# Six products a step instead of ten, and three reciprocals of a stage's four formed on ScalarE as exp(-ln)

## The chip, the cores and the metric

The kernel runs on one core of a Trainium2 chip, in one launch. The metric is the device time of that launch in microseconds (us), the median over several runs. The core has a matrix engine (PE, with its weight loads listed apart as PEld), VectorE (DVE), ScalarE (ACT), GpSimd (POOL), and SyncE (SP), which issues nearly all DMAs here. Each engine works through its own queue in order; they wait for one another by semaphores.

## The reference, cut to what matters

Input `A_x` is 2048 tokens by 640 features, 32 heads of 20. Two attention branches are computed from it and mixed by a per-token gate. The change lies in the first branch, A:

```python
qkv = (x @ wqkv) ...                       # q, k, v: 32 heads x 2048 tokens x 20
pq, pk = q @ w_phi, k @ w_phi              # per head, 20 x 20
phi_q = concat([softmax(pq), softmax(-pq)])   # 40 features of a head; phi_k likewise
kv  = einsum('sf,sd->fd', phi_k, v)        # 40 x 20 per head
z   = phi_k.sum(s)
num = phi_q @ kv                           # 2048 x 20 per head
den = phi_q @ z + 1e-6
a   = (num / den) @ wo
out = g * a + (1 - g) * b                  # g = sigmoid(x . gate_w); b is the second branch
```

Branch B is a causal attention in four segments of 512 tokens with a memory carried from one to the next. It comes after branch A's stage in the program and takes over half of the time.

## The kernel before, in words

The feature axis (640) is cut into five tiles of 128 rows, numbered j. A head has 20 rows, so heads straddle tiles: heads 6, 12, 19 and 25 have rows in two tiles. The 32 heads' results lie in two banks of PSUM, 16 heads (320 columns) each. `PIECES` (L63) lists the matmuls that put one row of heads together: (tile j, bank, first head, end head). Before, a head that two tiles share has a piece of its own (20 columns) in the second tile, so there are ten pieces, 36 heads' widths in all (720 columns). `FIRST` and `LAST` mark the pieces that open and close a bank.

`PIECES` is used in two places. `emit_foldM` (L186) folds `w_phi` into the key and query weights at the start of the program, five times for the keys (`WkA`) and five times for the queries (`WqA`). `emit_num` (L477) computes the numerators of 128 tokens ("chunk" `ch`, 16 of them) for one sign of the features (`sgn`, 2): 32 steps. A step's tile `num` has two banks; columns 0 to 319 of each hold the numerators. In the chunks 1, 5 and 9 the columns from 320 on also take the denominators of two later chunks (`emit_den`, L495: 20 small matmuls, 10 for each chunk), by both signs those of the next four chunks.

The stage around the change runs from about 88.8 to 127 us. Its order is written out by hand (a manual schedule). Four chunks are a batch; k is a chunk's place in it. For a step i = 2 ch + sgn, in the order of emission:

- DVE multiplies the numerators by a per-head factor into `tt` (`emit_tt`, L531). The factor of a batch's chunks is made one batch ahead.
- PE projects one half of a row of the second branch's keys, queries or values (`emit_half`, five matmuls of 320 columns, L561); ACT copies it out of PSUM (L621). There are two buffers for that (`pps`).
- PE computes the numerators of step i + 3 (L482), with denominators (L500) where they fall due. The three tiles `nps0`, `nps1`, `nps2` go round, so step i + 3 needs that everything which reads step i's tile is done.
- After both signs POOL adds the two halves of `tt` into `oA` (L691), and SP turns `oA` with a DMA. There are two `tt` tiles, so `tt` of chunk ch waits for `oA` of chunk ch - 2.

The factor of the next batch: on DVE, a reciprocal of one half of the denominators straight from PSUM into `rr` (L507) and a product with the other half into `uu` (L508), both right behind `tt` in the two steps of k = 1; the sum of `uu` over the signs, `dd` (L512), behind `tt` of step (k = 2, sign 0); at the end of k = 2 a reciprocal of `dd` (L694); then POOL multiplies by the gate (L522) and into `rr` (L524), behind `oA` of that chunk. The first batch's factor is made before the stage, from a tile `z_den`, in one piece (`first_chain`).

In chunks 1, 5, 9 and 11 ACT also starts exponential features of the keys (L706, L679, L681), which POOL adds two chunks later (L701).

Before the loop a short sequence fills the pipeline, L658: `"nnhhn"`, n for the numerators of the next step, h for a half. The stage's PSUM pools (`nps0`, `nps2`, `pps`, `nps1`, two banks each) take over the four two-bank tiles of the stage before, whose last work is a projection `pq` that ACT reads twice for its exponentials `Eq` (L428).

ACT loads its table of functions once, ahead of a dummy exponential (L132); until the end it runs exponentials, copies and Relu.

Of the kernel before, what the change touches and what calls it, by code (L numbers as in the profile page):

```python
# [7 lines left out]
ACT = mybir.ActivationFunctionType  # L8
ALU = mybir.AluOpType
BF16 = mybir.dt.bfloat16  # L10
F32 = mybir.dt.float32
# [4 lines left out]
def kernel(  # L16
# [15 lines left out]
    nc = tc.nc  # L32
    P = 128
    S = 2048
    D = 640
    H = 32
# [23 lines left out]


    TH = [(P * j // DH, (P * j + P - 1) // DH + 1) for j in range(KC)]
    PIECES = [(0, 0, 0, 7), (1, 0, 6, 7), (1, 0, 7, 13), (2, 0, 12, 13), (2, 0, 13, 16),  # L63
              (2, 1, 16, 20), (3, 1, 19, 20), (3, 1, 20, 26), (4, 1, 25, 26), (4, 1, 26, 32)]
    FIRST, LAST = {0, 5}, {4, 9}
    HW = 8

    gS = res.tile([P, NCH], F32, name="gS")
# [31 lines left out]
    for what in "c w1 w3 x0 x1 g v0 v1".split():  # L100
        n = int(what[1:]) if len(what) > 1 else 0
# [19 lines left out]
    for g in range(3):  # L121
# [7 lines left out]
                            compare_op=ALU.not_equal, fill=1.0, base=0,  # L129
                            channel_multiplier=1)  # L130
    nc.gpsimd.memset(tiny, 0.0)
    nc.scalar.activation(out=tiny, in_=tiny, func=ACT.Exp)  # L132
    wmask = Aw.tile([P, KC, H], F32, name="wmask")
    nc.gpsimd.memset(wmask, 1.0)
# [41 lines left out]
    def w2tile(name):  # L176
        return aps.tile([P, 2, 512], F32, name=name, tag="w2")
# [8 lines left out]
    def emit_foldM(WT, dst, ic, eng=nc.scalar.copy):  # L186
        ps = w2tile("fold_ps")
        for n, (j, bk, lo, hi) in enumerate(PIECES):
            h0 = TH[j][0]
            nc.tensor.matmul(ps[:, bk, (lo - 16 * bk) * DH:(hi - 16 * bk) * DH],  # L190
                             lhsT=WT[:, j, ic * P:(ic + 1) * P],
                             rhs=Wphi[:, j, lo - h0:hi - h0, :].rearrange("p h d -> p (h d)"),
                             start=(n in FIRST), stop=(n in LAST))
        eng(out=dst[:, ic, :].rearrange("p (b n) -> p b n", b=2), in_=ps[:, :, 0:320])

    def emit_xT(n):
# [120 lines left out]
    for step in "P T0a T2d M0a T1d M2a T4d T3d M1a X0 M4a X1 M3a k0 g k1 v0 v1 r0 r1".split():  # L317
        n = int(step[1:2] or 0)
# [29 lines left out]
    for n in range(KC):  # L348
# [12 lines left out]
        out=xg, in0=vA[:, :, 0, 320].rearrange("p (g u) -> p u g", u=4)[:, :, :, None].to_broadcast([P, 4, 4, 4]),  # L361
        in1=bd01[:, None, None, :].to_broadcast([P, 4, 4, 4]), op=ALU.mult)
# [101 lines left out]
    a3w = a3_stack.enter_context(tc.tile_pool(name="a3w", bufs=2, side="right", reuse_waits="tile"))  # L464
# [10 lines left out]
    NB = 4  # L475

    def emit_num(ch, sgn):  # L477
        qb, qc = divmod(ch, HB // P)
        t = nps[(2 * ch + sgn) % 3].tile([P, 2, 512], F32, name="num")
        for n, (j, bk, lo, hi) in enumerate(PIECES):  # L480
            h0 = TH[j][0]
            nc.tensor.matmul(t[:, bk, (lo - 16 * bk) * DH:(hi - 16 * bk) * DH],  # L482
                             lhsT=Eqs[qb, j][:, sgn, qc * P:(qc + 1) * P],
                             rhs=kvn[:, sgn, j, lo - h0:hi - h0, :].rearrange("p h e -> p (h e)"),
                             start=(n in FIRST), stop=(n in LAST))
        return t

    def num_view(t):
        return t[:, :, 0:320].rearrange("p b (h e) -> p b h e", e=DH)

    def den_view(t):

        return t[:, :, 320:448].rearrange("p n (s h e) -> p n s h e", s=2, e=2)
# [11 lines left out]
    def emit_rr(rr, uu, t, o, n):  # L505
        k = slice(o, o + n)
        nc.vector.reciprocal(out=rr[:, k], in_=t[:, :, :, :, 1])  # L507
        nc.vector.tensor_tensor(out=uu[:, k], in0=t[:, :, :, :, 0], in1=rr[:, k], op=ALU.mult)  # L508

    def emit_dsum(uu, n):  # L510
        dd = a3w.tile([P, NB, H], F32, name="dd", bufs=1)
        nc.vector.scalar_tensor_tensor(out=dd[:, 0:n], in0=uu[:, 0:n, 0, :], scalar=1e-6,  # L512
                                       in1=uu[:, 0:n, 1, :], op0=ALU.add, op1=ALU.add)
        return dd

    def rr_tiles():
        return (a3w.tile([P, NB, 2, H], F32, name="rr"), a3w.tile([P, NB, 2, H], F32, name="uu", bufs=1))

    def emit_cs(chs, rr, dd, o=0):
        n = len(chs)  # L520
        k = slice(o, o + n)
        nc.gpsimd.tensor_tensor(out=dd[:, k], in0=dd[:, k],  # L522
                                in1=gS[:, chs[0]:chs[0] + n, None].to_broadcast([P, n, H]), op=ALU.mult)
        nc.gpsimd.tensor_tensor(out=rr[:, k], in0=rr[:, k],  # L524
                                in1=dd[:, k, None, :].to_broadcast([P, n, 2, H]), op=ALU.mult)
        for i, ch in enumerate(chs):
            cs_of[ch] = rr[:, o + i]

    def emit_tt(tt, sgn, ps, cs):
        csb = cs[:, sgn].rearrange("p (b h) -> p b h", b=2)[:, :, :, None].to_broadcast([P, 2, 16, DH])  # L530
        nc.vector.tensor_tensor(out=tt[:, sgn].rearrange("p (b h) d -> p b h d", b=2),  # L531
                                in0=ps, in1=csb, op=ALU.mult)
# [52 lines left out]
    for what in "ppppvzppppdvp":  # L585
# [15 lines left out]
        name=n, bufs=2 if n == "pps" else 1, space=bass.MemoryType.PSUM, reuse_waits="tile"))  # L601
# [23 lines left out]
    def emit_turn(part, sc, dst):  # L625
        c = sc % 4
        nc.sync.dma_start_transpose(out=dst[:, :, c * P:(c + 1) * P],
                                    in_=stages[part][sc % 2].rearrange("p h e -> p (h e)"))
# [8 lines left out]
    def emit_next_half():  # L637
        if halves:
            emit_half(pps, *halves.pop(0), nc.scalar.copy)
# [10 lines left out]
    def emit_num_at(i):  # L650
        if i < len(order):
            ch, sgn = order[i]
            t = nums[ch, sgn] = emit_num(ch, sgn)
            if ch % 4 == 1 and ch < NCH - 4:
                for n in range(2):
                    emit_den(den_view(t)[:, n], ch + 3 + 2 * sgn + n)

    for what in "nnhhn":  # L658
        if what == "n":
            emit_num_at(len(nums))  # L660
        else:
            emit_next_half()
    for ch in range(NCH):
        bt = next(n for n, chs in enumerate(BATCH) if ch in chs)
        k = ch - BATCH[bt][0]
        ahead = BATCH[bt + 1] if bt < len(BATCH) - 1 else None
        tt = a3w.tile([P, 2, H, DH], F32, name="tt")
        for sgn in range(2):
            t = nums.pop((ch, sgn))
            emit_tt(tt, sgn, num_view(t), cs_of[ch])  # L670
            if ahead and sgn == 0 and k == 1:
                rr_n, uu = rr_tiles()
            if ahead and (k, sgn) in ((1, 0), (1, 1)):
                emit_rr(rr_n, uu, den_view(t), 2 * sgn, 2)
            for _ in range((ch, sgn) not in IDLE):
                emit_next_half()
            emit_num_at(2 * ch + sgn + 3)
            if ch - 1 in KEYS and sgn == 0:
                nc.scalar.activation(out=ek, in_=ek, func=ACT.Exp, scale=-1.0)  # L679
            elif ch - 1 in KEYS:  # L680
                nc.scalar.activation(out=phik, in_=key, func=ACT.Relu)  # L681
            if (ch, sgn) in EXPS:
                part = EXPS[ch, sgn]
                nc.scalar.activation(out=(phiks[1][:, 0] if part == "k" else phiq_st)[:, :, 0:DH],
                                     in_=stages[part][0][:, :, 0:DH], func=ACT.Exp)
            if (ch, sgn) in TWICE:
                emit_next_half()
            if ahead and k == 2 and sgn == 0:
                dd = emit_dsum(uu, NB)
        oA = a3w.tile([P, D], BF16, name="oA", bufs=4)  # L690
        nc.gpsimd.tensor_tensor(out=oA.rearrange("p (h d) -> p h d", d=DH),  # L691
                                in0=tt[:, 0], in1=tt[:, 1], op=ALU.add)
        if ahead and k == 2:
            nc.vector.reciprocal(out=dd, in_=dd)  # L694
            emit_cs(ahead, rr_n, dd)
        while turns_due:
            part, c = turns_due.pop(0)
            emit_turn(part, c, (kTs if part == "k" else qTs)[c // 4])
        nc.sync.dma_start_transpose(out=oTA[:, slot(ch)], in_=oA)
        if ch - 2 in KEYS:  # L700
            nc.gpsimd.tensor_tensor(out=phik, in0=phik, in1=ek, op=ALU.add)  # L701
        if ch in KEYS:
            key = stages["k"][KEYS[ch] % 2][:, :, 0:DH]
            phik = phiks[0][:, KEYS[ch], :, 0:DH]
            ek = a3w.tile([P, H, DH], BF16, name="ek")
            nc.scalar.activation(out=ek, in_=key, func=ACT.Relu, scale=-1.0)  # L706
# [5 lines left out]
    with ExitStack() as bctx:  # L712
# [6 lines left out]
            name=n, bufs=2 if n == "bps" else 1, space=bass.MemoryType.PSUM, reuse_waits="tile"))  # L719
# [480 lines left out]
        for ps, lo in quarters:  # L1200
            for k5 in range(KC):
                nc.tensor.matmul(ps, lhsT=oT4[:, 2, k5, :], rhs=WoB[:, k5, lo:lo + 160],
                                 start=(k5 == 0), stop=(k5 == KC - 1))
# [36 lines left out]
```

## Time and profile before

| | us |
|---|---|
| median of 3 runs (314.03 to 315.04) | 314.35 |
| the profiled execution | 314.52 |
| its span, first to last instruction | 312.8 |
| outside of the span (314.52 - 312.8) | 1.7 |
| PE, ACT, DVE, POOL busy | 302.4, 251.9, 230.3, 205.6 |
| granted TensorE clock | 1.0 |

Times in the views are microseconds from the start of the span, durations of single instructions often nanoseconds. "L482 PE num" is the numerators' matmuls, "L561 PE proj" the halves, "L531 DVE tt" the products, "L691 POOL oA" the sums, "L507 DVE rr" the reciprocals that the change moves, "L428 ACT Eq" the exponentials of the stage before, "L774 ACT PT" those of the second branch. In the timeline a line holds a start, a duration, an engine, a line, and the number of instructions that were merged; in the chain of waits each line is a piece of the chain that ended last.

### The profile page before, as it was taken

The page shows a single profiled execution, that of the slowest core. Times are in us where ns is not written, and L with a number is a line of the kernel's source. Part 1 is how long each engine was busy: PE and PEld are TensorE (multiplying, and loading weights), DVE is VectorE, ACT ScalarE, POOL GpSimd, SP SyncE. Part 2 cuts the span into 40 slices and gives each one's busy share as a digit, 9 for nine tenths or more (in the row PEclk, how much of TensorE's full clock was granted, in tenths as well). Part 3 has the DMA queues.
Part 4 walks back from the last instruction along what each step waited for, and adds up shares of the span by engine and source line. Part 5 has one row for each costly group of instructions (what it writes and reads, how often), then busy time and mean ns, then how long its engine had stood idle before and what let it go on. Part 6 is the DMA issues. An engine that isn't in the chain of part 4 may idle for free.

```text
span 312.8 us, 9844 instructions
## 1 busy us (share of the span) xinstructions
PE 302.4 (97%) x4038; PEld 205.3 (66%) x4038; DVE 230.3 (74%) x532; ACT 251.9 (81%) x320; POOL 205.6 (66%) x310
## 2 busy tenths in 40 slices
PE   8999999999999999999999999999999999999995
PEld 7788877855578788465656666666666666544573
DVE  3477997998779997767758588788656746667773
ACT  4677888357956549899999899999998999899953
POOL 8588599103346989965666667688886767756560
PEclk9999999999999999999999999999999999999999
DMA  7989934439217998775331358343855556334142
GB/s 223 202 173 188 234 103 127 130 88 365 76 27 99 129 142 132 153 103 105 37 69 36 69 111 121 57 91 61 110 92 90 53 106 116 82 82 97 40 115 84
DMA packets 97414, 35.33 MB, mean 113 GB/s; under 512 B 85722, under 2 KB 97370, under 8 KB 97370
## 3 DMA queue, kind: packets, MB, share of 16 engines
q1 hardware_dynamic: 96794, 34.06, 56.3%
q10 hardware_dynamic: 576, 0.66, 0.7%
q8 instruction: 31, 0.51, 0.7%
q14 instruction: 13, 0.11, 0.1%
HBM read 6.10 MB, written 2.62 MB: 28 GB/s over the span
## 4 chain that ended last, share of the span: by engine, by line
PE 68%; ACT 21%; DVE 5%; POOL 3%; issue 2%; ACTq 0%; DVEq 0%; POOLq 0%
ACT PT L774 18%; PE proj L1008 10%; PE st_ps L770 9%; PE proj L948 8%; PE pq L421 7%; PE pk L240 7%; PE pv L240 7%; PE nda L824 5%; PE proj L561 3%; DVE tt L531 2%; PE num L482 2%; PE kv_ps L394 2%; DVE rr L507 2%; POOL oA L691 1%; PE warm L316 1%
## 5 line engine op out<-in xcount | busy, mean ns | idle before, releaser
L774 ACT ACTIVATE PT<-st_ps 128x1024 bf16<-128x1024 f32 x160 | 153.9, 1024 | 11.3 <-PE st_ps L770 8.9
L781 POOL TENSOR_SCALAR_AFFINE_SELECT PT<-PT 128x512 bf16<-128x512 bf16 (+1 forms) x130 | 83.8, 663 | 42.7 <-ACT PT L774 42.3
L259 POOL TENSOR_TENSOR EkSn<-Ek,krec 128x1280 bf16<-128x1280 bf16 x15 | 35.1, 2358 | 9.2 <-DVE krec L258 7.3
L824 PEld LDWEIGHTS <-PT 128*128 128x128 bf16 x1040 | 32.9, 96 | 7.8 <-issue 4.5
L1008 PEld LDWEIGHTS <-xTf 128*128 128x128 bf16 x300 | 26.5, 97 | 14.1 <-issue 5.5
L824 PE MATMUL nda<-vB,PT 128*128 128x21 bf16 x1000 | 34.2, 173 | 0.0
L1014 DVE CAST Z<-proj 128x320 bf16<-128x320 f32 x44 | 21.2, 489 | 16.4 <-PE proj L1008 15.3
L428 ACT ACTIVATE Eq<-pq 128x1024 bf16<-128x1024 f32 x20 | 19.4, 1021 | 12.6 <-PE pq L421 12.6
L255 DVE TENSOR_REDUCE ksum<-Ek 128x64 f32<-128x1280 bf16 x16 | 23.6, 1475 | 7.2 <-ACT Ek L251 7.2
L948 PE MATMUL proj<-WkA,oTA 128*128 128x320 bf16 x160 | 28.3, 300 | 0.0
L531 DVE TENSOR_TENSOR tt<-num,rr 128x640 f32<-128x640 f32 x32 | 25.0, 813 | 4.4 <-POOL rr L524 1.7
L770 PE MATMUL st_ps<-Z 32*128 32x512 bf16 (+3 forms) x256 | 25.2, 299 | 3.0 <-ACT PT L774 2.5
L691 POOL TENSOR_TENSOR oA<-tt 128x640 bf16<-128x640 f32 x16 | 24.6, 1546 | 5.2 <-DVE tt L531 5.0
L770 PE MATMUL st_ps<-Eq 32*128 32x384 bf16 (+3 forms) x256 | 25.6, 298 | 1.9 <-ACT PT L774 1.5
L251 ACT ACTIVATE Ek<-pk 128x640 bf16<-128x640 f32 x32 | 20.8, 703 | 8.1 <-PE pk L240 7.0
L240 PEld LDWEIGHTS <-xTf 128*128 128x128 bf16 x200 | 22.6, 113 | 4.7
L421 PE MATMUL pq<-xTf,WqA 128*128 128x512 bf16 x100 | 22.4, 379 | 0.3 <-issue 0.3
L948 PE MATMUL proj<-WvA,oT 128*128 128x320 bf16 x120 | 21.2, 300 | 0.0
L948 PEld LDWEIGHTS <-oTA 128*128 128x128 bf16 x160 | 13.5, 97 | 8.6 <-issue 4.6
L561 PEld LDWEIGHTS <-xTf 128*128 128x128 bf16 x180 | 15.8, 97 | 4.6
L770 PEld LDWEIGHTS <-Z 32*128 32x128 bf16 x256 | 7.5, 91 | 16.2 <-issue 15.0
L482 PEld LDWEIGHTS <-Eq 128*128 128x128 bf16 x320 | 15.9, 96 | 3.3 <-issue 0.7
(194 smaller groups left out, 584.8 us busy)
## 6 DMA issues: line engine op xcount, KB each, us to landing
Z<-EkSn SPq DMA_DIRECT2D x32, 160.0 KB, 2.8
out_dram<-orow SPq DMA_DIRECT2D x8, 160.0 KB, 1.8
out_dram<-oTA SPq DMA_DIRECT2D x6, 160.0 KB, 1.8
WvA<-in_A_wqkv_dram SPq DMA_DIRECT2D x2, 400.0 KB, 5.9
WvB<-in_B_wv_dram SPq DMA_DIRECT2D x1, 800.0 KB, 4.6
WkB<-in_B_wk_dram SPq DMA_DIRECT2D x1, 800.0 KB, 6.4
WqB<-in_B_wq_dram SPq DMA_DIRECT2D x1, 800.0 KB, 8.1
WkA<-in_A_wo_dram SPq DMA_DIRECT2D x1, 800.0 KB, 11.2
```

The source lines that it names most:

```text
L240: nc.tensor.matmul(ps[:, bk, 0:n], lhsT=key_tokens(c, sc), rhs=rhs, start=(c == 0), stop=(c == by_row[-1][0] if sc == 0 and W is WkA else ...
L259: (nc.vector if sc == NCH - 1 else nc.gpsimd).tensor_tensor(out=EkSn[:, sc].rearrange("p s (h f) -> p (s h) f", f=DH), in0=Ek.rearrange("p ...
L421: nc.tensor.matmul(pq[:, half, :], lhsT=WqA[:, c, j * P:(j + 1) * P], rhs=xq[:, 2 * qb + half, c], start=(c == 0), stop=(c == KC - 1))
L531: nc.vector.tensor_tensor(out=tt[:, sgn].rearrange("p (b h) d -> p b h d", b=2), in0=ps, in1=csb, op=ALU.mult)
L561: nc.tensor.matmul(ps, lhsT=xq[:, sc // 4, cc, sc % 4 * P:(sc % 4 + 1) * P], rhs=W[:, cc, half * 320:(half + 1) * 320], start=(cc == 0), s ...
L691: nc.gpsimd.tensor_tensor(out=oA.rearrange("p (h d) -> p h d", d=DH), in0=tt[:, 0], in1=tt[:, 1], op=ALU.add)
L770: nc.tensor.matmul(ps[:, i - i0, o:o + L - c * P], lhsT=kT[32 * i:32 * i + 32, c * P:(c + 1) * P], rhs=qT[32 * i:32 * i + 32, c * P:L], st ...
L774: nc.scalar.activation(out=PT[:, i0:i0 + 2], in_=ps, func=ACT.Exp, scale=SCALE_B)
L781: nc.gpsimd.affine_select(out=v, in_=v, pattern=[[0, n_i], [1, P]], compare_op=ALU.is_ge, fill=0.0, base=0, channel_multiplier=-1)
L824: nc.tensor.matmul(nd[:, j, i], lhsT=block(st, c)[:, i, (j - c) * P:(j - c + 1) * P], rhs=vB[:, c, 4 * st.g + i, :], start=(c == 0), stop= ...
L948: nc.tensor.matmul(ps, lhsT=oT[:, k % KC], rhs=W[:, k % KC, hs], start=(k == 0), stop=(k == n - 1))
L1008: nc.tensor.matmul(ps, lhsT=xq[:, sc // 4, k, sc % 4 * P:(sc % 4 + 1) * P], rhs=W[:, k, half * 320:(half + 1) * 320], start=(k == 0), stop ...
```

## The change

Four edits, in one diff:

1. `PIECES` has six entries, one for each tile and bank. A tile's matmul covers all its heads of a bank, adding on the columns of the head that it shares with the tile before and writing the others. The columns are the same 720, in six matmuls instead of ten, in `emit_num` and `emit_foldM`.
2. ACT's table is named before the dummy exponential, a set that holds both the exponential and the logarithm.
3. The order before the loop is `"nnnhh"`: three numerators, then two halves.
4. In the two steps of k = 1, ACT copies both halves of the denominators from PSUM into a new SBUF tile `sd`, takes the logarithm of one half into `rr`, and then exp(-x) in place. DVE's product `uu` reads `sd` and `rr` and comes behind `tt` in the two steps of k = 2; `dd` follows in step (k = 2, sign 1). The first batch's chain and the reciprocal of `dd` stay on DVE.

```diff
-    PIECES = [(0, 0, 0, 7), (1, 0, 6, 7), (1, 0, 7, 13), (2, 0, 12, 13), (2, 0, 13, 16),
-              (2, 1, 16, 20), (3, 1, 19, 20), (3, 1, 20, 26), (4, 1, 25, 26), (4, 1, 26, 32)]
-    FIRST, LAST = {0, 5}, {4, 9}
+    PIECES = [(0, 0, 0, 7), (1, 0, 6, 13), (2, 0, 12, 16), (2, 1, 16, 20), (3, 1, 19, 26), (4, 1, 25, 32)]
+    FIRST, LAST = {0, 3}, {2, 5}
...
+    nc.scalar.preload_act_table_set("natural_log_exp_and_others")
     nc.scalar.activation(out=tiny, in_=tiny, func=ACT.Exp)
...
-    for what in "nnhhn":
+    for what in "nnnhh":
...
             if ahead and sgn == 0 and k == 1:
                 rr_n, uu = rr_tiles()
+                sd = a3w.tile([P, NB, 2, H, 2], F32, name="sd", bufs=1)
             if ahead and (k, sgn) in ((1, 0), (1, 1)):
-                emit_rr(rr_n, uu, den_view(t), 2 * sgn, 2)
+                two = slice(2 * sgn, 2 * sgn + 2)
+                nc.scalar.copy(out=sd[:, two], in_=den_view(t))
+                nc.scalar.activation(out=rr_n[:, two], in_=sd[:, two, :, :, 1], func=ACT.Ln)
+                nc.scalar.activation(out=rr_n[:, two], in_=rr_n[:, two], func=ACT.Exp, scale=-1.0)
+            if ahead and (k, sgn) in ((2, 0), (2, 1)):
+                two = slice(2 * sgn, 2 * sgn + 2)
+                nc.vector.tensor_tensor(out=uu[:, two], in0=sd[:, two, :, :, 0], in1=rr_n[:, two], op=ALU.mult)
...
-            if ahead and k == 2 and sgn == 0:
+            if ahead and (k, sgn) == (2, 1):
                 dd = emit_dsum(uu, NB)
```

The matmuls of both users of `PIECES` also get a flag for the program's own group check, which is no instruction.

## The prediction

> **What bounds the kernel now.** First the page's shares, then the busy times of each engine in the stage that the change touches.
>
> ```profile
> span 312.8 us, 9844 instructions
> PE 302.4 (97%) x4038; PEld 205.3 (66%) x4038; DVE 230.3 (74%) x532; ACT 251.9 (81%) x320; POOL 205.6 (66%) x310
> 92.00:102.00 10.00, 10.00 (x167) 8.30 (x164) 9.23 (x14) 5.32 (x11) 6.28 (x7) 1.00 0.68 99
> 102.00:112.00 10.00, 9.92 (x165) 8.16 (x164) 9.36 (x15) 5.32 (x11) 9.55 (x12) 1.00 0.93 138
> ```
>
> In the windows the columns are PE, PEld, DVE, ACT, POOL. PE, DVE and (from 102 on) POOL are all over 90% busy; ACT alone has room, 4.7 us in ten. So nothing taken from one of the three pays in full, and ACT is where work can go. Third, the chain of waits from 86 to 135 us:
>
> ```profile
> 102.06 0.82 DVE tt L531
> 102.89 0.88 DVE rr L507
> 103.79 0.29 DVE uu L508
> 104.08 0.73 DVE tt L531
> 104.81 0.87 DVE rr L507
> 105.71 0.30 DVE uu L508
> 106.05 0.54 PE num L482 x10
> 106.60 0.68 PE proj L561 x5
> ...
> 129.44 4.37 ACT PT L774 x5
> ```
>
> In k = 1 DVE's reciprocals carry the end; PE waits for the second `uu`, which reads the PSUM tile that step i + 3 wants. At 129.44 the chain is on ACT's exponentials of branch B: what the stage gains or loses goes on as a shift. Fourth, the timeline where the stage begins:
>
> ```profile
> 89.01 1.94 ACT L428 ACTIVATE Eq<-pq 128x1024 bf16<-128x1024 f32 x2 [1.41 <-PE pq L421]
> 89.58 1.52 PE L561 MATMUL proj<-WkB,xTf 128*128 128x320 bf16 x10
> 91.00 0.54 PE L482 MATMUL num<-kvn,Eq 128*128 128x140 bf16 x10
> ```
>
> The third numerators start 0.05 after the last exponentials end (89.01 + 1.94 = 90.95), and 0.06 later than behind five L561 matmuls alone (two halves of 0.68 from 89.58 end at 90.94). The stage's eight banks are the four tiles of the stage before; numerators 0 and 1 and the halves all start before 90.95, so `nps2`, step 2's, must be the one that ACT still reads. Today two halves fill that time.
>
> **Fewer matmuls.** Ten pieces take 0.384 us (in the chain, L482 x10 between halves is 0.38): short ones start 0.026 apart whatever their width, 80 columns 0.035, 140 columns 0.060. Six make 4 x 0.060 + 2 x 0.035 = 0.311. So 32 x 0.073 = 2.3 us of PE. The key folds gain 3 x 0.073 = 0.2 (the first two run at half clock, where the columns set the time: 0.62 for 720); PE runs on from them to 52 us, so I take 0.2, between 0 and 0.2. The query folds lie behind ACT's copies (L194, 54.0 to 57.1): nothing.
>
> **The table.** One load either way, 1.28 us at 2.2, in front of a wait for the first data: nothing.
>
> **Order "nnnhh".** Step 2 is asked for at 88.81 + 2 x 0.311 = 89.43 and can't start before 91.00. PE stands for 1.57 us, and the two halves, 2 x 0.68 = 1.36, come after. Queued behind them: every half and numerator.
>
> **The chain to ACT.** Nearest rows for ACT: 0.20 (one element), 0.23 (32), 0.43 (320). So a copy of 256 about 0.37, and twice 0.31 for 128: 1.0 us in each of six steps (bounds 3 x 0.20 and 3 x 0.43). The idle ACT hides it (L621 waits 7.4 + 6.5 us for PE). Behind it in ACT's queue is the next half's copy, for which PE waits two halves later, 1.3 us after the half's end, of which the copy needs 0.43.
>
> DVE loses six L507 at 0.98 from start to next. The `uu` move, behind `tt` of k = 2. Each reads two tiles in SBUF, where before one operand lay in PSUM. Two views show what that means:
>
> ```profile
> L508 DVE TENSOR_TENSOR uu<-num,rr x6: 291/291/291, 93.9 to 115.7; 128x128 f32<-128x128 f32 x6
> 187.40 0.19 DVE L895 TENSOR_TENSOR rec<-rec,Eq 128x32 f32<-128x32 f32 x1
> 295.76 0.87 POOL L867 TENSOR_TENSOR oB<-td 128x320 bf16<-128x320 f32 x1 [1.38 <-DVE td L857]
> 295.98 0.70 DVE L895 TENSOR_TENSOR rec<-rec,Eq 128x32 f32<-128x32 f32 x1
> ```
>
> L508, with one operand in PSUM, takes 291 ns whether `oA` runs or not. L895, with two in SBUF, takes 0.19 alone and 0.70 beside a POOL instruction: it ends 0.05 after it (296.68 against 296.63). So a DVE instruction with two SBUF operands waits for the running POOL one. `oA` takes 1.55. Of an L895 beside POOL the rows show waits from 0 to 0.5; nine instructions are exposed (six `uu`, three `dd`), so the bounds are 0 (no gain: nothing waits for the port now) and 9 x 1.55 = 14 us of DVE. I take the place where each falls.
>
> The Trainium skill says this as a rule ("SBUF — State Buffer", Who interferes with whom): a DVE instruction with two SBUF inputs contends with a GpSimd one that reads SBUF, and the loser blocks until the other's whole instruction is done. By it the price is that of the walk below; by the L895 waits alone (up to 0.5 each) most of it would fit in DVE's slack and the sum would be near 315. The trace's L895 agrees with the whole wait, but shows none as long as an `oA`.
>
> **The walk, first batch** (starts; before in brackets). Step 2 ends with its denominators 91.0 + 0.31 + 0.52: `tt` 2 at 92.0 [92.15]. Halves 0 to 2 and step 3 with denominators: 91.83 + 2.03 + 0.83 = 94.70, `tt` 3 at 94.9 [94.08]. A half and a numerator on, `tt` 4 at 95.9 [96.0]. The two reciprocals saved have paid for the start, no more. POOL runs `oA` 1 from 95.8 to 97.35. ACT's first chain, behind a half's copy that ends 95.9, is done at 97.0; the first `uu` waits for the port until 97.35. `tt` 5 runs 97.4 to 98.2, and frees `oA` 2, 98.27 to 99.8. The second chain ends at 98.26, so the second `uu` finds the port taken and ends at 99.9; `dd` 100.2, reciprocal 101.2, `tt` 6 and 7, and `tt` 8 at 102.6 [100.56]: 2.0 late, 1.3 of it by the port.
>
> **Second and third batch.** `tt` 8 to 16 and 16 to 24 take 9.93 each before. DVE's own list after: eight `tt` at 0.743, two `uu` at 0.2 to 0.3, `dd` 0.3, reciprocal 0.86 = 7.6. PE needs 8 x (0.68 + 0.31) + 2 x 0.52 = 8.95, so without the port PE would set the pace, 1.0 less a batch. With it DVE waits about 0.6 for the first `uu` (it comes in the middle of an `oA`) and 1.4 for `dd` or the second `uu` (the `oA` that `tt` 5 releases takes the port first), and with the denominators' wait ahead of the second `tt` of k = 1 and POOL's queue (L701 1.35, then `oA`) the same walk gives 10.0 and 10.8: `tt` 24 at 123.4 [120.43].
>
> **Last batch.** POOL sets it: `oA` 11 behind `tt` 23 (123.45), L701, `oA` 12 till 127.9, which lets `tt` 28 go [124.74]. Numerators 31 wait for that tile, the last half is copied at 129.96 [126.88]. Stage B starts 3.0 late.
>
> **Sum.** 314.5 (profiled) - 0.2 + 3.0 = 317.3; the profiled run lies 0.17 over the median of 314.35, so 317.2.
>
> **Rivals.**
>
> *The tensor engine sets the pace.* The port never binds, because `uu` and `dd` fall between POOL's instructions, and step 2's tile is free early: then 2.3 of PE count, less 0.8 that POOL (8.45 a batch: four `oA` at 1.5, 0.5, 0.7, 1.3) and the denominators' waits keep: 1.5. 314.35 - 0.2 - 1.5 = 312.7. It decides if DVE's waits stay under 1.3 a batch and numerators 2 start before 90. For it: PE's waits in the stage are short (0.2 for `uu`). Against: `oA` is running, or released by the very `tt` ahead, wherever the new list has a two-operand instruction. 0.14.
>
> *Start lost, port free.* The walk without port waits gives `tt` 8 at 101.3, `tt` 24 at 120.1, the last copy at 126.6, 0.25 early: 314.35 - 0.45 = 313.9. 0.14.
>
> *Port in part:* `dd` slips in ahead of `oA`; some 1.4 a batch less in two of three, 315.3 to 316. 0.08.
>
> *Worse:* the table is reloaded between logarithm and exponential: twelve loads of 1.28 on ACT, 5 us a batch where 4.7 in ten are free, with PE's halves behind; 319 to 325. Or ACT falls two copies behind in k = 1, where L706 (0.74) joins. 0.06. The Trainium skill ("ScalarE: Activation LUTs", Table sets) lists a set with both functions, one load; no run here shows it yet.
>
> **Chances and range.** The forecast has 0.58, alone 316.0 to 318.5. A measurement here tells about 0.3%, 0.94 us: faster under 313.4, slower over 315.3. Slower 0.58 + 0.08 + 0.06 = 0.72, same 0.14, faster 0.14. The range leaves out the fastest and the worst: 313.8 to 318.8.
>
> **What would show it.** A PE wait of about 1.5 us for L428 before numerators 2. L482 x192 with 0.31 a step. The new `uu` at 0.8 to 1.6 us beside `oA` and 0.28 alone; `dd` over 1 us. L507 once. One table load. The first L774 near 130. I am wrong if `uu` and `dd` stay at 0.28 beside `oA` (port), if numerators 2 start near 89.4 (start), or if stage B's length changes by more than 0.5 us (shift).

## The result, and the profile after

The changed kernel takes 316.88 us, the median of six runs (316.74 to 317.36), against 314.27 for the kernel before: a ratio of 1.0084, with a 95% interval of 1.0060 to 1.0108. The profiled execution took 316.90, with a span of 315.2. Line numbers have moved a little: `tt` is now L534, `uu` L685, `dd` L515, `oA` L702, the numerators L484, the halves L564, the last exponentials of the stage before L430, ScalarE's three steps L680 to L682.

The page first, then the same windows as before (the length of the window, then PE, PEld, DVE, ACT, POOL):

```profile
span 315.2 us, 9521 instructions
PE 299.4 (95%) x3866; PEld 201.5 (64%) x3870; DVE 231.2 (73%) x526; ACT 255.6 (81%) x338; POOL 205.9 (65%) x310
```

```profile
92.00:102.00 10.00, 8.82 (x126) 7.11 (x125) 8.42 (x11) 6.57 (x17) 5.68 (x5) 1.00 0.74 128
102.00:112.00 10.00, 8.32 (x104) 6.52 (x102) 8.58 (x12) 6.15 (x16) 8.49 (x11) 1.00 0.83 123
```

PE has 3.0 us less to do and yet the span is longer: in these windows PE was 99 to 100% busy and is now at 83 to 88%. DVE has lost six reciprocals of 0.88, over 5 us, and its busy time over the span went up by 0.9. A busy time that rises while work leaves points to instructions that stand still while they hold their engine. The timeline of the second batch shows which one, first DVE, then POOL:

```profile
105.07 0.83 DVE L534 TENSOR_TENSOR tt<-num,rr 128x640 f32<-128x640 f32 x1 [0.79 <-POOL oA L702]
105.81 0.88 DVE L685 TENSOR_TENSOR uu<-sd,rr 128x128 f32<-128x128 f32 x1
106.61 0.81 DVE L534 TENSOR_TENSOR tt<-num,rr 128x640 f32<-128x640 f32 x1
107.35 0.28 DVE L685 TENSOR_TENSOR uu<-sd,rr 128x128 f32<-128x128 f32 x1
107.66 1.54 DVE L515 SCALAR_TENSOR_TENSOR dd<-uu 128x128 f32<-128x128 f32 x1
109.23 0.95 DVE L705 RECIPROCAL dd<-dd 128x128 f32<-128x128 f32 x1
110.10 3.02 DVE L534 TENSOR_TENSOR tt<-num,rr 128x640 f32<-128x640 f32 x4
```

```profile
103.50 3.04 POOL L702 TENSOR_TENSOR oA<-tt 128x640 bf16<-128x640 f32 x2
107.50 1.55 POOL L702 TENSOR_TENSOR oA<-tt 128x640 bf16<-128x640 f32 x1 [0.96 <-DVE tt L534]
```

The first `uu` falls into an `oA` that runs until 106.54 and ends 0.15 after it. The second one starts at 107.35, in the gap between two `oA`, and takes its 0.28. `dd` needs the result of that `uu`, so it can start only at 107.66; the `oA` that `tt` released has begun at 107.50, and `dd` ends at 109.20, again 0.15 after `oA` (109.05). Its work is 0.28. Meanwhile `tt`, with one operand in PSUM, keeps its length beside `oA` (0.83 for the one at 105.07, which lies within the second `oA` of POOL's first line, 105.00 to 106.54). Over the three batches the six `uu` took 0.47, 0.29, 0.88, 0.28, 0.88 and 0.27, and the three `dd` 1.52, 1.54 and 1.54. In the first batch the second `uu` and an `oA` start almost together:

```profile
96.36 0.29 DVE L685 TENSOR_TENSOR uu<-sd,rr 128x128 f32<-128x128 f32 x1
96.37 1.69 POOL L702 TENSOR_TENSOR oA<-tt 128x640 bf16<-128x640 f32 x1 [0.96 <-DVE tt L534]
```

Here it is POOL that is held up: this `oA` takes 1.69, where the others take 1.54 or 1.55. This agrees in full with the rule that the prediction named from the Trainium skill ("SBUF — State Buffer", Who interferes with whom).

Who pays is in the waits of the stage (who waited for whom: us in total, how often, the longest) and in PE's timeline:

```profile
PE num L484 <- DVE tt L534: 4.2, 3, 1.5
PE proj L564 <- ACT Eq L430: 0.6, 1, 0.6
```

```profile
99.93 0.48 PE L484 MATMUL num<-kvn,Eq 128*128 128x140 bf16 x6 [1.10 <-DVE tt L534]
110.92 0.48 PE L484 MATMUL num<-kvn,Eq 128*128 128x140 bf16 x6 [1.54 <-DVE tt L534]
121.90 0.47 PE L484 MATMUL num<-kvn,Eq 128*128 128x140 bf16 x6 [1.53 <-DVE tt L534]
```

Three waits, one for each batch: behind `dd` stand its reciprocal and the `tt` that frees the numerators' tile. Before, PE waited 0.2 in all on that side. ScalarE's new steps are in the chain of waits too, though the list of waits doesn't name them. From the second batch:

```profile
104.57 0.28 ACT sd L680
...
105.50 0.41 ACT Z L624
105.91 0.28 ACT sd L680
106.19 0.04 issue
106.24 0.47 PE num L484 x6
```

The numerators of step i + 3 go into the tile that the copy `sd` reads. They start 0.99 after the five halves ahead of them (105.25), where 0.68 is usual: about 0.3 in each of the two later batches. The kernel before lost 0.24 at this place to its second `uu`. At the end of the stage the loss goes on whole:

```profile
129.43 1.94 ACT L785 ACTIVATE PT<-st_ps 128x1024 bf16<-128x1024 f32 x2
```

Before, this line stood at 127.21. From there to the end of the span both kernels need the same, 185.6 and 185.8.

The starts of the stage differ from one profiled execution to the next, so the kernels are compared below by stretches that begin with the first numerators (88.81 before, 87.72 after). The stage is the time from those to the first `PT`; the middle columns are the first sums of a batch, `tt` 0, 8, 16 and 24, from start to start. All are differences of starts in the traces.

| kernel | median | ratio (95%) | numerators 0 to `tt` 8 | 8 to 16 | 16 to 24 | stage |
|---|---|---|---|---|---|---|
| before | 314.27 | | 11.75 | 9.94 | 9.93 | 38.40 |
| changed | 316.88 | 1.0084 [1.0060, 1.0108] | 12.81 | 11.05 | 10.99 | 41.72 |
| e1: six pieces alone | 313.61 | 0.9983 [0.9964, 1.0002] | 11.69 | 9.92 | 9.92 | 38.23 |
| e2: ScalarE's chain alone | 318.53 | 1.0153 [1.0121, 1.0185] | 13.77 | 11.05 | 10.98 | 43.10 |
| e3: changed, old order | 317.97 | 1.0126 [1.0095, 1.0157] | 13.64 | 11.05 | 10.97 | 42.54 |
| e4: changed, `dd` unblocked | 314.22 | 1.0004 [0.9989, 1.0020] | 11.70 | 10.69 | 9.71 | 38.97 |
| e5: changed, `dd` and `uu` unblocked | 313.42 | 0.9977 [0.9957, 0.9996] | 11.70 | 10.06 | 9.09 | 37.74 |
| e6: changed, one `uu` | 316.81 | 1.0082 [1.0060, 1.0104] | 12.74 | 10.84 | 10.77 | 41.23 |
| e8: before, new order | 314.95 | 1.0031 [1.0013, 1.0049] | 12.70 | 9.98 | 9.93 | 39.38 |
| e9: before, `dd` later | 314.04 | 1.0004 [0.9988, 1.0021] | 11.55 | 10.27 | 9.73 | 38.59 |
| e10: chain straight from PSUM | 314.40 | 1.0011 [0.9998, 1.0024] | 12.53 | 10.32 | 9.49 | 39.05 |
| e11: e10, new order | 313.87 | 0.9989 [0.9976, 1.0002] | 11.70 | 10.31 | 9.47 | 38.19 |
| e12: before, table line | 315.29 | 1.0046 [1.0031, 1.0062] | 13.11 | 9.93 | 9.92 | 39.73 |
| e13: e1, table line, new order | 313.31 | 0.9979 [0.9961, 0.9998] | 11.74 | 9.94 | 9.92 | 38.30 |

Each ratio is to runs of the kernel before on the same chip (medians 313.89 to 314.27).

### The profile page after: what moved, and what is told of

It is laid out like the page before. It is cut to its first block, busy times and chain, and to the rows that moved or that the text cites. A ratio compares the mean times of both kernels' runs of the same rounds, so it can differ in the third digit from the quotient of the medians.

```text
span 315.2 us, 9521 instructions
## 1 busy us (share of the span) xinstructions
PE 299.4 (95%) x3866; PEld 201.5 (64%) x3870; DVE 231.2 (73%) x526; ACT 255.6 (81%) x338; POOL 205.9 (65%) x310
## 4 chain that ended last, share of the span: by engine, by line
PE 66%; ACT 23%; DMA 4%; issue 3%; DVE 2%; POOL 1%; ACTq 0%; SPq 0%; DVEq 0%
ACT PT L785 18%; PE proj L1019 10%; PE st_ps L781 10%; PE proj L959 8%; PE pq L423 7%; PE pk L242 6%; PE pv L242 6%; PE nda L835 5%; PE proj L564 5%; DMA xTf<-in_A_x_dram 3%; PE num L484 2%; PE kv_ps L396 2%; DMA wnat_k<-in_A_wqkv_dram 1%; PE v_ps L564 1%; PE nda L844 1%
## 5 line engine op out<-in xcount | busy, mean ns | idle before, releaser
L534 DVE TENSOR_TENSOR tt<-num,rr 128x640 f32<-128x640 f32 x32 | 24.9, 813 | 6.9 <-PE num L503 3.1
L430 ACT ACTIVATE Eq<-pq 128x1024 bf16<-128x1024 f32 x20 | 19.4, 1021 | 12.3 <-PE pq L423 12.3
L702 POOL TENSOR_TENSOR oA<-tt 128x640 bf16<-128x640 f32 x16 | 24.7, 1553 | 5.7 <-DVE tt L534 5.5
L564 PEld LDWEIGHTS <-xTf 128*128 128x128 bf16 x180 | 16.2, 98 | 5.3 <-issue 0.7
L484 PE MATMUL num<-kvn,Eq 128*128 128x140 bf16 (+1 forms) x192 | 15.0, 216 | 4.5 <-DVE tt L534 4.2
```

The source lines that it names most:

```text
L564: nc.tensor.matmul(ps, lhsT=xq[:, sc // 4, cc, sc % 4 * P:(sc % 4 + 1) * P], rhs=W[:, cc, half * 320:(half + 1) * 320], start=(cc == 0), s ...
```

## The experiments

The theory: DVE instructions with two operands in SBUF stand while POOL's `oA` runs, and this is the whole loss. The rivals: the order at the start (numerators 2 waiting for ScalarE), ScalarE's longer list holding up the copies of the halves, and the pieces.

**e1, the pieces alone.** The kernel before with this edit only:

```diff
-    PIECES = [... ten ...]
-    FIRST, LAST = {0, 5}, {4, 9}
+    PIECES = [(0, 0, 0, 7), (1, 0, 6, 13), (2, 0, 12, 16), (2, 1, 16, 20), (3, 1, 19, 26), (4, 1, 25, 32)]
+    FIRST, LAST = {0, 3}, {2, 5}
```

> The kernel before with the six pieces alone (old order before the loop, all reciprocals on DVE). Port theory (the loss comes from DVE's two-operand instructions): nothing of that is here, so no loss; PE has 32 x 0.073 = 2.3 us less to do, but in three batches of four DVE's reciprocals carry the end, so the stage from numerators 0 to the last half's copy gets 0.2 to 0.8 shorter: 313.5 to 314.3. Product theory (adding and writing in one matmul is itself slower, or the pieces make the stage's matmuls wait): a step's six matmuls take over 0.38 and the time is above 314.6.

Measured: 313.61, a ratio of 0.9983, and a stage of 38.23, 0.17 shorter. PE's 2.3 us of freed time bring almost nothing, since the chain of this kernel is still DVE's reciprocals with POOL behind:

```profile
91.33 0.82 DVE tt L532
92.16 0.88 DVE rr L508
93.06 0.29 DVE uu L509
```

**e2, the chain on ScalarE alone**: edits 2 and 4 of the change, with ten pieces and the old order.

```diff
+    nc.scalar.preload_act_table_set("natural_log_exp_and_others")
...
-                emit_rr(rr_n, uu, den_view(t), 2 * sgn, 2)
+                ... copy, Ln, Exp on nc.scalar; uu at (2, 0) and (2, 1); dd at (2, 1)
```

> The kernel before with ACT's logarithm and exponential and the moved uu and dd alone (ten pieces, old order). Port theory: dd lasts about 1.5 us in each of three batches and uu 0.3 to 0.9, PE waits over 1 us a batch for tt, and all of the loss is here: 316.5 to 318. Start theory (the new order before the loop costs as much as the port): about half of the loss, 315 to 316.

Measured: 318.53, over the range of either theory and slower than the whole change. The loss is therefore in this part, and the other two edits give something back: with six pieces as well (e3) the stage is 0.56 shorter, with the new order too (the changed kernel) another 0.82. The blocked instructions are the same here (`dd` 1.52 to 1.55, `uu` up to 0.85). But not all of the 4.70 by which this stage is longer comes from them: the edits include the line for the table set, which alone makes the stage of the kernel before 1.33 longer (e12 below).

**e3, the changed kernel with the old order.**

```diff
-    for what in "nnnhh":
+    for what in "nnhhn":
```

> The changed kernel with the old order before the loop (two numerators, two halves, one numerator). Start theory: PE's 0.58 us wait for the last exponentials of the stage before goes, and numerators 3 start 0.45 earlier against the stage's start: 316.88 - 0.45 = 316.4. Port theory with slack: the first batch is held by the first dd anyway, so the gain shrinks to 0 to 0.3: 316.6 to 316.9.

Measured: 317.97, 1.1 slower than the changed kernel. So the new order helps there, against the prediction and against both theories of this expectation. The reason is in PE's timeline, where it is the halves that wait for ScalarE's last exponentials, not numerators 2. First e3, then the changed kernel:

```profile
90.34 1.52 PE L564 MATMUL proj<-WkB,xTf 128*128 128x320 bf16 x10 [1.40 <-ACT Eq L430]
```

```profile
87.72 1.11 PE L484 MATMUL num<-kvn,Eq 128*128 128x140 bf16 x18
89.91 1.52 PE L564 MATMUL proj<-WkB,xTf 128*128 128x320 bf16 x10 [0.58 <-ACT Eq L430]
```

With three numerators first (x18 is three steps of six), they and the denominators fill most of the time that the halves must wait anyway.

**e4, `dd` with one operand.** The changed kernel, where `dd` is a reduction over `uu`, read as one operand in SBUF. It leaves out the 1e-6.

```diff
-                dd = emit_dsum(uu, NB)
+                dd = a3w.tile([P, NB, H], F32, name="dd", bufs=1)
+                nc.vector.tensor_reduce(out=dd, in_=uu.rearrange("p n s h -> p n h s"), axis=AX.X, op=ALU.add)
```

> The changed kernel with dd formed by a reduction over uu, which reads one SBUF operand instead of two (the 1e-6 is left out of the later batches' sums); what it waits for and where it stands in DVE's queue are unchanged. Port theory: dd takes 0.3 to 0.5 us beside a running oA instead of 1.5, PE's waits of 1.1, 1.5 and 1.5 us for tt shrink under 0.5 each, and the time falls by 2 to 3.5: 313.4 to 315. Queue theory (the place of uu and dd behind tt of k = 2 and ACT's chain set the delay, not the port): dd still ends as late, and the time stays over 316.3.

Measured: 314.22, that is 2.66 less than the changed kernel, for one instruction in a batch. DVE and then POOL in the second batch:

```profile
105.86 0.28 DVE L685 TENSOR_TENSOR uu<-sd,rr 128x128 f32<-128x128 f32 x1
106.17 0.42 DVE L701 TENSOR_REDUCE dd<-uu 128x128 f32<-128x256 f32 x1
```

```profile
106.01 1.54 POOL L703 TENSOR_TENSOR oA<-tt 128x640 bf16<-128x640 f32 x1 [0.96 <-DVE tt L534]
```

At the same place, beside an `oA` that has just begun, the reduction takes 0.42. It reads both halves of `uu` through one operand (256 columns) and isn't held up: in e6, with no `oA` running, the same reduction takes 0.43. PE's waits for `tt` fall from 4.2 to 1.4. The Trainium skill says in the same section that a `tensor_reduce` never contends with GpSimd on trn2; the 0.42 agrees.

**e5, `uu` with one operand too.** As e4, and `uu` is a reduction of `rr` over an axis of one, with the product left out: an output of the same size, one operand.

```diff
-                nc.vector.tensor_tensor(out=uu[:, two], in0=sd[:, two, :, :, 0], in1=rr_n[:, two], op=ALU.mult)
+                nc.vector.tensor_reduce(out=uu[:, two], in_=rr_n[:, two, :, :, None], axis=AX.X, op=ALU.add)
```

> The changed kernel in which neither uu nor dd reads two SBUF operands: dd as in the run with the reduction, and uu a one-operand reduction over the exponential's result (the product with the other half of the denominators and the 1e-6 are left out of the later batches' factors). Places in the queue and waits are unchanged. Port theory: uu near 0.3 us in all six steps, against 0.88 in two of them, so 0.2 to 1.0 under the run with the reduction alone (314.2): 313.2 to 314.0. Queue theory: no difference, 314.0 to 314.5.

Measured: 313.42. All six `uu` take 0.28 or 0.29, and PE waits 0.2 for `tt`. From the changed kernel to this one the stage loses 1.11, 0.99 and 1.90 in its three batches, and 3.98 in all (41.72 to 37.74): without the blocked instructions the change would have been 0.66 faster in the stage than the kernel before, and 0.7 by the median. The blocked instructions cost more than the whole difference between the two kernels, so the rest of the change is a gain on balance. Single terms in it may still be losses: PE still stands 0.3 a batch for the copy `sd` (numerators at 105.19, the halves ahead of them from 104.22), and the halves still wait 0.58 at the start.

**e6, one `uu` instead of two**, behind the second `tt` of k = 2, with `dd` as in e4.

```diff
-            if ahead and (k, sgn) in ((2, 0), (2, 1)):
-                ... uu[:, two] ...
+            if ahead and (k, sgn) == (2, 1):
+                nc.vector.tensor_tensor(out=uu, in0=sd[:, :, :, :, 0], in1=rr_n, op=ALU.mult)
```

> The changed kernel with the two uu in one instruction behind tt of step (k = 2, sign 1), so that it is issued ahead of the oA which that tt releases, and dd as a reduction (the 1e-6 is left out). Correct sums otherwise. Port theory, issue order decides: uu takes about 0.45 us unblocked, oA of k = 2 is held 0.2 to 0.3 instead, and the time is that of the run without two-operand instructions within 0.4: 313.2 to 314.2. If POOL wins the port: uu near 1.9 us and 315 to 316.

Measured: 316.81, no better than the changed kernel and over both ranges; the single instruction did not slip in ahead of `oA`. DVE, then POOL:

```profile
95.94 1.32 DVE L684 TENSOR_TENSOR uu<-sd,rr 128x256 f32<-128x256 f32 x1 [0.57 <-ACT rr L682]
```

```profile
95.45 1.54 POOL L702 TENSOR_TENSOR oA<-tt 128x640 bf16<-128x640 f32 x1 [0.46 <-DVE tt L534]
```

Here `uu` waits 0.57 for ScalarE, `oA` starts meanwhile, and `uu` ends behind it. In the other two batches it waits 0.29 and 0.30 for ScalarE and takes 1.62 and 1.60. In this place waits of 0.29 to 0.57 were enough to lose to POOL each time.

**e8, the new order in the kernel before.**

```diff
-    for what in "nnhhn":
+    for what in "nnnhh":
```

> The kernel before with the new order before the loop alone. As predicted: numerators 2 wait for the last exponentials, halves 0 and 1 come after, and the stage gets up to 1.36 us longer; DVE's reciprocals carry the first batch, so 0.5 to 1.4: 314.4 to 315.3. Layout theory (the banks go to whichever pool is used last before the loop): the halves wait instead, 0.5 us, and the time is within 0.4 of before.

Measured: 314.95, a ratio of 1.0031, the stage 0.98 longer:

```profile
89.66 0.54 PE L482 MATMUL num<-kvn,Eq 128*128 128x140 bf16 x10 [1.26 <-ACT Eq L428]
```

In this kernel the wait is where the prediction put it (1.26, where it had 1.57). The reading of the tile was right for the kernel before, and not for the changed one.

**e9, `dd` moved in the kernel before**, behind the second `tt` of k = 2, where the change has it, with nothing else.

```diff
-            if ahead and k == 2 and sgn == 0:
+            if ahead and (k, sgn) == (2, 1):
                 dd = emit_dsum(uu, NB)
```

> The kernel before with dd behind tt of step (k = 2, sign 1) instead of sign 0, all else as before (two-operand dd, DVE reciprocals). Port theory, issue order decides: dd does not wait for anything but the queue, so it is issued ahead of the oA that the same tt releases; dd stays near 0.28, oA is held 0.1 to 0.2, time within 0.4 of before. If a two-operand instruction loses to oA wherever both come due: dd 1.5 us three times, and 316 to 318.

Measured: 314.04, the same as before. `dd` has two operands in SBUF and stands at the same place as in the changed kernel, and yet takes 0.28. DVE, then POOL:

```profile
96.70 0.28 DVE L512 SCALAR_TENSOR_TENSOR dd<-uu 128x128 f32<-128x128 f32 x1
```

```profile
96.86 1.54 POOL L691 TENSOR_TENSOR oA<-tt 128x640 bf16<-128x640 f32 x1 [1.10 <-DVE tt L531]
```

Here `uu` is long done, so `dd` follows `tt` at once and is 0.16 ahead of the `oA` that the same `tt` releases. In the changed kernel the second `uu` took that gap, and `dd`, which needs its result, came 0.16 after `oA` in the second batch. Place and operands are alike; who starts first decides between 0.28 and 1.54.

**e10 and e11, ScalarE's chain without a copy.** The kernel before with six pieces and the line for the table set; ScalarE takes the logarithm straight from PSUM as soon as the denominators are there, and `uu` stays behind `tt` of k = 1, with one operand in PSUM. e11 has the new order besides.

```diff
+                rr_a, two = ahead_tiles[-1][0], slice(2 * sgn, 2 * sgn + 2)
+                nc.scalar.activation(out=rr_a[:, two], in_=den_view(t)[:, :, :, :, 1], func=ACT.Ln)
+                nc.scalar.activation(out=rr_a[:, two], in_=rr_a[:, two], func=ACT.Exp, scale=-1.0)
...
-                emit_rr(rr_n, uu, den_view(t), 2 * sgn, 2)
+                nc.vector.tensor_tensor(out=uu[:, two], in0=den_view(t)[:, :, :, :, 0], in1=rr_n[:, two], op=ALU.mult)
```

> The kernel before with six pieces, and with the reciprocals of the stage's 28 later chunks on ScalarE, by logarithm and exponential, taken straight from the PSUM tile as soon as its denominators are there; uu stays where it was, behind the sums of k = 1, and reads one operand in PSUM and one in SBUF; dd stays behind the first sums of k = 2. DVE thus loses six reciprocals (0.88 each) and gains no instruction with two SBUF operands. If the blocked instructions are the cause (my theory): uu 0.27 to 0.30 in all six places, dd 0.28 or, where an oA is still running, up to 0.9; PE sets the pace of the stage (some 9.0 to 9.3 for eight sums where before has 9.93), and the time is 312.2 to 313.3. Rival, that the cost of the change comes from ScalarE's extra instructions standing ahead of the copies of the halves: they are still there (0.31 + 0.31 a tile, with a wait for the denominators), so the time would be 314 to 316.

> The same with three numerators ahead of the two halves at the start of the stage. If the banks lie as in the kernel before (numerators 2 in the banks that ScalarE's last exponentials read), numerators 2 wait 1.2 to 1.6 us for these and the time is 0.3 to 1.0 over that of the first of the two; if they lie as in the changed kernel (the halves in those banks), the halves wait about 0.6 and the time is 0.5 to 1.1 under it.

Measured: 314.40 and 313.87; e10 misses its range by 1.1 and falls into that of its rival. Right of it: the six `uu` take 0.28 each, `dd` 0.87 to 0.92, and in e11 the order is worth 0.5, at the lower end of what the banks of the changed kernel would give. Wrong was that PE would set the pace alone. In e11 the stage is only 0.2 shorter than before although DVE has lost six reciprocals and PE 2.3 us. The chain of waits of its second batch shows what comes next:

```profile
99.41 1.55 POOL oA L701
100.96 0.60 POOL Z L711
101.56 0.66 issue
102.22 1.55 POOL oA L701
103.77 0.02 issue
103.80 0.82 DVE tt L533
104.62 0.79 DVE dd L514
...
107.70 0.42 POOL Eq L743
108.12 0.36 POOL Eq L769
108.48 0.36 POOL dd L524
...
109.03 0.74 POOL rr L526
```

POOL: four sums at 1.5, 1.3 for the keys' features, 1.1 for the factor, and in this batch 1.1 more (L743, L769, L771) for the second branch, ahead of the factor for which `tt` 16 waits. `dd` is still held up by 0.6 in between. Removing DVE's work leaves POOL's list at the same length. Against the rival of ScalarE's longer list stand two runs: e11 has the same list as e10 and is 0.5 faster by the order alone, and e5, with the copies `sd` besides, takes 313.42.

**e12, the line for the table set in the kernel before.**

```diff
+    nc.scalar.preload_act_table_set("natural_log_exp_and_others")
     nc.scalar.activation(out=tiny, in_=tiny, func=ACT.Exp)
```

> The kernel before with one line more: the table set is loaded by name ahead of the first exponential. The program has one instruction more on ScalarE, at 2 us, and does the same work. In the built program the last tile of the first branch's q products has moved from banks 2 and 3 (nps2, the numerators of step 2) to banks 4 and 5 (pps, the two halves). If the bank that ScalarE's last exponentials read decides who waits at the start of the stage: the halves wait about 1.3 us for them, numerators 2 stand behind the halves, the first exponential of branch B comes about 0.7 to 1.1 us later after the first numerators, and the time is 314.8 to 315.3. Rival, that it was the six pieces or ScalarE's longer list that moved the wait in the changed kernel: the halves run at once as before, and the time is that of before within 0.3.

Measured: 315.29, a ratio of 1.0046, and a stage 1.33 longer, at the work of the kernel before:

```profile
89.81 1.52 PE L562 MATMUL proj<-WkB,xTf 128*128 128x320 bf16 x10 [1.26 <-ACT Eq L429]
```

Two orders and two places for the last `pq` tile give a table of the stage: halves first 38.40 (tile in the numerators' banks) and 39.73 (in the halves' banks); numerators first 39.38 and, with six pieces, 38.30. The order that fits costs nothing, the other one about 1 us. The runs show that the wait moves with the line for the table set, from numerators 2 (e8) to the halves (e12). That the tile has moved to other banks is read from the built program; why this line moves it is not shown.

**e13, that line and the new order, with six pieces and the reciprocals on DVE.** The edits are those of e1, e12 and e8.

> The kernel before with the named table set, six pieces and three numerators ahead of the halves, but with the reciprocals on DVE and uu and dd where they were. By the bank theory numerators 2 run at once and the halves wait 0.5 to 0.7; DVE, which sets the pace here, gets its third sums about 1.5 earlier after the first numerators and keeps what of it the reciprocals leave: 0.6 to 1.2 less from the first numerators to the first exponential of branch B, and 312.9 to 313.6. Rival, that DVE's list from the first sums to the eighth is full anyway: within 0.3 of the kernel before.

Measured: 313.31, with a stage of 38.30 against 38.23 in e1. The halves wait 0.58, as the bank theory has it, and the time lies in its range, but the rival was right on the stage: `tt` 8 comes 11.74 after the first numerators, as before. Of the versions that leave nothing out it has the lowest ratio, 0.9979 (0.9961 to 0.9998), which can't be told from the 0.9983 of e1 and hardly from no change.

## Why the prediction was right or wrong

**The time and its sign: right, in part by luck.** Forecast 317.2, measured 316.88. The profiled times add up: the start of the stage 1.09 earlier, the stage 3.32 longer (forecast 3.0), the rest 0.17 longer, together 2.4, from 314.52 to 316.90. Two things made the number better than the working. Inside the stage a term that was too heavy (the start) and one that was too light (the second batch) nearly cancel. And the start of the stage, forecast 0.2 earlier, came 1.09 earlier in the profiled execution, by a spread between executions (last section) that was not foreseen.

**The port: right in kind, near in size.** Waits "about 0.6 for the first `uu`" and "1.4 for `dd` or the second `uu`": in the second and third batch 0.60 and 1.26, always `dd`. In the first batch the walk had the second `uu` stand for most of an `oA`; there `uu` waited 0.19 and `dd` 1.24. By batch the walk put the port at 1.3, 1.05 (10.0 - 8.95) and 1.85 (10.8 - 8.95); taking it away (e5) gives 1.11, 0.99 and 1.90. The walk of the rival with a free port gives less, 3.3 at `tt` 24 (123.4 - 120.1), since it counts 9.4 for each of the two later batches where the other has 8.95. With e5 they take 10.06 and 9.09, and the stage falls by 3.98.

**The start: wrong.** The step reads "`nps2`, step 2's, must be the one that ACT still reads", and takes it over to the changed kernel. It is true of the kernel before (e8). But with the change's line for the table set, costed at nothing, the wait moves to the halves (e12). Numerators 2 ran at once, 0.63 after the first, which is the 89.4 that the prediction named as its sign of a wrong start, and the halves waited 0.58. Of the 2.0 forecast for `tt` 8, 1.3 was the port and 0.7 the start; measured were 1.06 in all, and without the port (e5) nothing is left. The order, forecast as a loss, gains 0.82 of the stage in the changed kernel (e3).

**The second batch: too light by 1.05** (11.05 against 10.0), the third too light by 0.2. What the walk had too small is the time that DVE stands idle ahead of the blocked instructions. Beside DVE's list of 7.6 and the port's 0.6 and 1.4, its 10.0 leaves 0.4 for that; in the trace it is 1.35, of which `tt` 12 waits 0.79 for an `oA`. POOL starts that `oA` only behind its sum for the keys' features (L712, 1.34). In the third batch it is 1.28, and there the walk's 10.8 left 1.2. In e5, without the port, the second batch takes 10.06 and the third 9.09, where the walk let PE set a pace of 8.95. There `tt` 16 waits 0.54 for its factor, ahead of which POOL has L745, L771 and L773 (1.1 together) in that batch alone. In the changed kernel these cost nothing, since POOL waits 0.33 for DVE's reciprocal behind them.

**The pieces: right in the duration, nearly right in the effect.** The chain has numerators of a step at 0.32, forecast 0.31. e1 gives 0.17 in the stage where DVE sets the pace. e3 against e2 gives 0.56, of which 0.13 lies before `tt` 8 and 0.42 behind `tt` 24. The 0.2 of the folds can't be told apart: the first numerators start between 87.3 and 88.8 in the traces, 87.9 on average over the five with ten pieces and 87.8 over the nine with six. That the first two folds are slower than the others is not so in every execution: in that of the changed kernel all five take 0.25 to 0.27 from the first start to the last.

**ScalarE: right in the durations, not quite in the effect.** Copy 0.38, logarithm 0.32, exponential 0.31, where 0.37 and twice 0.31 were forecast; one table load, 1.28. This bears out the set with both functions that the prediction named from the Trainium skill ("ScalarE: Activation LUTs", Table sets). "The idle ACT hides it" leaves out the 0.3 a batch that PE stands for the copy `sd`.

**The rivals.** "The tensor engine sets the pace" gave 312.7 without the port. With the port away (e5) the time is 313.42. PE is 97 to 99% busy there from 92 to 122 us, so it does set the pace, as that rival had it. The waits for `sd` (0.3 a batch), at the start (0.58) and for POOL's factor are seen in its trace, but what each is worth was not tried.

## What to carry to other kernels

Moving work off a busy engine moves its operands too. Here an operand that went from PSUM into SBUF made a `uu` of 0.28 us take up to 0.88 beside GpSimd's `oA`. Moving it also changes who comes first: `dd` had both operands in SBUF before as well, and most of the loss (2.7 us by e4, 0.8 more by e5) came from its new place behind a `uu`. So look for each two-operand instruction at who starts first: the `dd` that followed its release at once got in ahead of `oA` (e9, 0.28), the ones that waited for a result on that place did not (1.54 in the changed kernel, 1.32 to 1.62 in e6); a reduction, with one operand, passed beside `oA` in 0.42 (e4). And a line that costs nothing by itself can change which instructions wait for a tile (e12), so an order that was written out for one program has to be read again in the new trace.

## What the runs showed of the hardware that was not expected

A blocked instruction ends 0.15 after the GpSimd instruction (109.20 against 109.05 for `dd`, 106.69 against 106.54 for `uu`, both of 128 columns), where the nearest row of the prediction, of 32 columns, had 0.05. The `uu` of 256 columns in e6 ends 0.28 after (97.27 against 96.99). The more columns, the later it ends, as if its work began only when POOL was done; no run was made to test that.

Kernels that are the same up to the first numerators start them at 88.81 (before), 87.47 (e8) and 88.05 (e9), in one profiled execution each. The 1.09 by which the changed kernel's stage starts earlier lies within that and is no effect of the change that could be shown. Much of the spread is there at the very start: from first start to last, PE's first two folds took 0.56 and 0.59 in the execution of the kernel before and 0.35 and 0.33 in that of e8, at a granted clock that reads 1.00, and the first products of the keys follow at 9.34 and 8.57. Over the 14 traces, late products of the keys mostly go with late numerators; what makes the folds slow in some executions was not tried.
